# Attention and a bilinear feed-forward on one core: transposes moved from TensorE to DMA

## The chip, the cores and the metric

The kernel runs on one core of a Trainium2 chip. The metric is device time in microseconds (us), the median of several executions. The profiler takes one execution; its span is about 2 us shorter than the measured time.

## The reference

Attention with a bias from a table of relative positions, then a feed-forward layer that multiplies two projections:

```
# q, k, v: [batch 8, heads 8, seq 576, dim 64];  w_a, w_b: [512, 1536];  w_out: [1536, 512]
scores = q @ k.T / 8 + bias[head, |i - j| bucket]
x      = softmax(scores) @ v              # back to [8 * 576, 512]
out    = ((x @ w_a) * (x @ w_b)) @ w_out  # float32
```

## The kernel before

A step of the main loop handles one pair of heads: 32 pairs, four to a batch. A sequence of 576 is 512 main positions and a tail of 64. While pair `s` is computed, `quota` units of feed-forward work for an earlier batch are put between its steps. A unit is four matrix products of 512 columns (0.216 us each); 36 units make a chunk of 512 rows, one chunk to a batch and a ninth one for all tails.

Each pair needs its queries and keys with the head dimension on partitions. TensorE transposes them: four blocks and a tail block for the queries, four blocks for the keys. Five more blocks turn the output of the previous pair into the layout of the feed-forward. VectorE copies every result out of PSUM.

```python
ps_sc (2 x 2 banks: scores)   ps_av (1 bank)   ps_tr (1 bank: transposes, tail product)
ps_ff (2 banks: feed-forward)
...
def t_q(p, eng=None):
    ps = ps_tr.tile([128, 1024], BF16, tag="tr", name=f"trq{p}")
    transposes(ps, qn, p, "qr")                       # 4 blocks on TensorE
    nc.tensor.transpose(ps[:, SM:SM + 128], qkt[b % 2][:, 2 * hp:2 * hp + 2, :], ident[:, :])
    copy(eng, qT[:, 0:S], ps[:, 0:S])                 # and four small copies of tails
...
def ff_a(c, df):                                      # one unit
    pa = ps_ff.tile([128, 512], FP32, tag="ffn", name=f"pa{c}_{df}")
    ... 4 products ...
    nc.scalar.activation(out=ha[:, :], in_=pa[:, :], func=ACTF.Copy)
def ff_b(c, df):                                      # the next unit
    pb = ps_ff.tile([128, 512], FP32, tag="ffn", name=f"pb{c}_{df}")
    ... 4 products ...
    nc.vector.tensor_tensor(out=g_sb[df][:, :], in0=pb[:, :], in1=ff["ha"][:, :], op=MULT)
...
quotas = {4: 7, 5: 7, 6: 7, 7: 8, 8: 7}               # 9 from pair 9 on
# one pair (U = a unit, A = attention times values of the pair before):
[qk(s,0), ex(s,0), U, ex(s,1), A(0,1,2), U, mul(s,0), t_q(s+1), U, mul(s,1), qk(s,2), ex(s,2), U,
 ex(s,3), t_k(s+1), U, mul(s,2), A(3,4), U, mul(s,3), qk_tail(s), ex_tail(s), U, t_x(s-1), U,
 mul_tail(s), U];  v_next(s)
```

Here `qk` is scores, `ex` their exponentials (ScalarE), `mul` the multiplication by the bias factor (VectorE), `t_q`, `t_k` and `t_x` the transposes of queries, keys and outputs, and `v_next` the copy of the next values (VectorE).

The softmax here doesn't subtract the row's maximum and nothing guards it: scores larger than these inputs give would overflow.

## Time and profile before

| | before |
|---|---|
| time, median of 3 | 450.67 us (449.96 to 452.07) |
| TensorE busy | 424.7 us, 95% of the span |
| VectorE, ScalarE busy | 64%, 55% |
| period of a batch in the middle | 47.52 us |

The first fence is from the page of the kernel before: busy time by engine, then the span in 40 slices with busy shares in tenths, the granted TensorE clock, and the DMA engines.

```profile
...
PE 424.7 (95%) x3578; PEld 221.1 (49%) x3643; DVE 287.4 (64%) x838; ACT 245.8 (55%) x350; POOL 88.9 (20%) x117
...
PE   5676999999999999999999999999999999999995
...
PEclk8579999999999999999999999999999999999999
DMA  9999999420942097207912290200010002002004
...
```

TensorE is at 9 (90% or more) in nearly every slice after the first four, at full clock. The DMA engines are idle for much of the middle.

The next fence is the stretch table of the kernel before. Columns: stretch, its length, busy time (count) of TensorE, weight loads, VectorE, ScalarE, GpSimd, then clock, DMA share (packet time over the time of 16 engines; packets overlap, so it can pass 1) and GB/s.

```profile
...
0.00:20.00 20.00, 10.97 (x51) 4.12 (x52) 11.78 (x50) 9.44 (x13) 14.71 (x25) 0.70 1.07 153
20.00:40.00 20.00, 14.80 (x187) 10.48 (x188) 15.15 (x55) 14.69 (x21) 10.47 (x15) 0.78 1.37 203
40.00:75.00 35.00, 32.35 (x321) 17.58 (x326) 30.03 (x90) 22.40 (x33) 19.58 (x24) 1.00 1.68 161
...
157.00:184.00 27.00, 26.74 (x256) 14.66 (x259) 19.84 (x56) 16.01 (x22) 9.28 (x11) 1.00 0.88 75
184.00:211.00 27.00, 26.79 (x247) 14.23 (x250) 18.94 (x57) 17.14 (x24) 4.96 (x7) 1.00 0.24 40
...
```

The first 40 us are start-up, where TensorE is busy about half of the time. In the middle it is busy 26.7 of 27 us.

The timeline of TensorE in the kernel before shows what a transpose costs. Columns: start, duration, engine, line, operation, output and inputs, shapes, count.

```profile
...
189.32 0.38 PE L426 MATMUL po_3_2890<-wo,g_127 128*128 128x512 bf16 x1
189.54 0.44 PE L395 MATMUL trx_2895<-ident,XG_112 128*128 128x128 bf16 x5
189.82 0.38 PE L426 MATMUL po_3_2890<-wo,g_128 128*128 128x512 bf16 x1
...
194.86 0.39 PE L262 MATMUL trq_2986<-ident,qn_93 128*128 128x128 bf16 x4
195.08 0.22 PE L268 MATMUL trq_2986<-ident,qkt_99 128*128 128x128 bf16 x1
195.14 0.38 PE L406 MATMUL pa_1_2997<-xn_120,wa_113 128*128 128x512 bf16 x1
...
```

Read start to start, because matrix products overlap: five output transposes take TensorE from 189.54 to 189.82, 0.28 us, and four query blocks and a tail block from 194.86 to 195.14, again 0.28 us. Four key blocks take 0.22 us. There is no idle time around them. The Trainium skill's page "TensorE: Matmul & The Clock Gate" (section "Wait — 56ns, not 53.3ns?") gives 55 to 56 ns between 128-column products; this trace agrees (0.28 us for five).

### The profile page before, as it was taken

What the parts mean: (1) busy time and instruction counts of PE and PEld (TensorE: products, weight loads), DVE (VectorE), ACT (ScalarE), POOL (GpSimd) and SP (SyncE); (2) the same over time, 40 slices, a digit from 0 to 9 for tenths busy, and PEclk for the clock granted to TensorE, in tenths of its full rate; (3) what the DMA queues carried; (4) which work ended last, traced back from release to release, by engine and by line L of the source; (5) the groups of instructions that cost most, each with busy time, mean ns of one, the idle gap of its engine ahead of it and who ended that gap; (6) DMA issues with size and microseconds to landing.
All of it is one profiled execution on the core that took longest, in us unless ns stands there. A gap on an engine that the chain in (4) does not pass through costs nothing.

```text
span 449.3 us, 9012 instructions
## 1 busy us (share of the span) xinstructions
PE 424.7 (95%) x3578; PEld 221.1 (49%) x3643; DVE 287.4 (64%) x838; ACT 245.8 (55%) x350; POOL 88.9 (20%) x117
## 2 busy tenths in 40 slices
PE   5676999999999999999999999999999999999995
PEld 2264455555555555555555555555555554444442
DVE  5579789668766787577856786587658862330320
ACT  2678566556655665566556665566556652322321
POOL 9456365010801070105200350100000000000000
PEclk8579999999999999999999999999999999999999
DMA  9999999420942097207912290200010002002004
GB/s 101 219 200 203 192 148 76 82 65 1 107 72 63 15 84 72 77 25 49 104 49 54 16 137 27 76 1 1 23 71 2 1 1 94 1 0 93 1 1 94
DMA packets 87370, 30.35 MB, mean 68 GB/s; under 512 B 64760, under 2 KB 82712, under 8 KB 87328
## 3 DMA queue, kind: packets, MB, share of 16 engines
q0 software_dynamic: 80144, 18.88, 45.0%
q1 hardware_dynamic: 6992, 10.86, 7.3%
q8 instruction: 28, 0.46, 0.4%
q14 instruction: 14, 0.11, 0.1%
q10 hardware_dynamic: 192, 0.03, 0.0%
HBM read 39.18 MB, written 9.45 MB: 108 GB/s over the span
## 4 chain that ended last, share of the span: by engine, by line
PE 83%; DVE 10%; DMA 3%; issue 2%; ACT 1%; SPq 0%; DVEq 0%; ACTq 0%
DMA Wt<-bias_tab 2%; DVE XG_111 L387 1%; DVE g_125 L419 1%; DVE g_124 L419 1%; PE warm L208 1%; PE po_1_1335 L426 1%; PE po_0_1275 L426 1%; DMA bias_tab<-tab_sb 1%; PE po_1_2057 L426 1%; PE po_1_4869 L426 1%; PE po_1_3463 L426 1%; PE po_1_2760 L426 1%; PE po_1_4166 L426 1%; PE po_2_1403 L426 1%; PE po_3_6071 L426 1%
## 5 line engine op out<-in xcount | busy, mean ns | idle before, releaser
L416 PEld LDWEIGHTS <-wb_118 128*128 128x128 bf16 x144 | 12.4, 97 | 16.6 <-issue 5.6
L406 PEld LDWEIGHTS <-wa_114 128*128 128x128 bf16 x144 | 12.5, 98 | 15.3 <-issue 3.4
L416 PEld LDWEIGHTS <-wb_117 128*128 128x128 bf16 x144 | 12.4, 97 | 14.9 <-issue 4.7
L406 PEld LDWEIGHTS <-wa_113 128*128 128x128 bf16 x144 | 12.5, 98 | 14.6 <-issue 3.0
L416 PEld LDWEIGHTS <-wb_116 128*128 128x128 bf16 x144 | 12.3, 97 | 14.9 <-issue 5.1
L406 PEld LDWEIGHTS <-wa_115 128*128 128x128 bf16 x144 | 12.7, 98 | 13.4 <-issue 2.5
L123 POOL DMA_DIRECT2D qn_93<-in_q_dram x12 | 11.0, 925 | 38.6 <-PE trq_3162 L268 18.5
L123 POOL DMA_DIRECT2D qn_94<-in_q_dram x12 | 10.6, 886 | 40.2 <-PE trq_2459 L268 18.5
L146 POOL DMA_DIRECT2D vt_104<-in_v_dram x8 | 4.9, 620 | 53.7 <-PE av_3_2848 L376 17.3
L132 POOL DMA_DIRECT2D kn_95<-in_k_dram x12 | 10.6, 906 | 6.8 <-DVE qr_844 L251 6.6
L146 POOL DMA_DIRECT2D vt_103<-in_v_dram x8 | 5.0, 640 | 34.8 <-PE av_3_2145 L376 17.3
L132 POOL DMA_DIRECT2D kn_96<-in_k_dram x12 | 10.6, 912 | 0.0
L395 PEld LDWEIGHTS <-XG_112 128*128 128x128 bf16 x80 | 5.8, 98 | 5.4 <-DVE XG_112 L387 1.5
L395 PEld LDWEIGHTS <-XG_111 128*128 128x128 bf16 x80 | 5.8, 98 | 5.1 <-DVE XG_111 L387 1.8
L302 PEld LDWEIGHTS <-KT_108 64*128 64x128 bf16 x88 | 2.8, 95 | 10.7 <-issue 8.6
L419 DVE TENSOR_TENSOR g_124<-pb_0_5871,ha_0_5869 128x512 bf16<-128x512 f32 x1 | 0.7, 692 | 11.4 <-PE pb_0_5871 L416 11.4
L302 PEld LDWEIGHTS <-KT_109 64*128 64x128 bf16 x88 | 2.6, 95 | 10.4 <-issue 10.4
L426 PEld LDWEIGHTS <-g_124 128*128 128x128 bf16 x36 | 3.5, 97 | 7.0 <-issue 4.7
L302 PEld LDWEIGHTS <-KT_110 64*128 64x128 bf16 x80 | 2.4, 95 | 8.2 <-issue 8.1
L114 POOL DMA_DIRECT2D vn_98<-in_v_dram x5 | 4.2, 836 | 7.4 <-DVE vm_102 L291 6.8
L426 PEld LDWEIGHTS <-g_126 128*128 128x128 bf16 x36 | 3.5, 98 | 4.3
L426 PEld LDWEIGHTS <-g_134 128*128 128x128 bf16 x36 | 3.5, 98 | 4.3
(3194 smaller groups left out, 1643.6 us busy)
## 6 DMA issues: line engine op xcount, KB each, us to landing
qn_93<-in_q_dram POOLq DMA_DIRECT2D x16, 128.0 KB, 4.2
kn_95<-in_k_dram POOLq DMA_DIRECT2D x16, 128.0 KB, 5.1
qn_94<-in_q_dram POOLq DMA_DIRECT2D x16, 128.0 KB, 5.4
kn_96<-in_k_dram POOLq DMA_DIRECT2D x16, 128.0 KB, 4.9
wo<-in_moe_w_out_dram POOLq DMA_DIRECT2D x1, 1536.0 KB, 16.4
vn_97<-in_v_dram POOLq DMA_DIRECT2D x3, 512.0 KB, 7.1
vn_98<-in_v_dram POOLq DMA_DIRECT2D x3, 512.0 KB, 5.8
vn_97<-in_v_dram POOLq DMA_DIRECT2D x2, 256.0 KB, 10.7
```

Source lines behind the costliest of these rows:

```text
L114: nc.gpsimd.dma_start(out=dst[:, 256 * h0:256 * h1].rearrange("p (h x) -> p h x", x=256), in_=src[b, h0:h1, 0:SM, :].rearrange("h (p t) d ...
L123: nc.gpsimd.dma_start(out=qn[b % 2][:, :].rearrange("p (t h d) -> p t h d", h=H, t=NM)[:, t, h0:h1, :], in_=q[b, h0:h1, 128 * t:128 * t + ...
L132: nc.gpsimd.dma_start(out=kn[b % 2][:, :].rearrange("p (t h d) -> p t h d", h=H, t=NM)[:, t, h0:h1, :], in_=k[b, h0:h1, t:SM:NM, :].transp ...
L146: nc.gpsimd.dma_start(out=vt[b % 2][64 * hh:64 * hh + 64, :, hh, 0:Dh], in_=v[b, hh:H:2, SM:S, :].transpose([1, 0, 2]))
L208: nc.tensor.matmul(out=warm[:, :], lhsT=zero_sb[:, 0:128], rhs=zero_sb[:, :], start=True, stop=True)
L302: nc.tensor.matmul(out=ps[:, hh, :], lhsT=kT[r, 128 * t:128 * t + 128], rhs=qT[r, 0:SM], start=True, stop=True)
L387: nc.vector.tensor_tensor(out=xg[0:np_, j0:j0 + n, :, :], in0=pav[0:np_, s0:s0 + n, :, 0:Dh], in1=rc.unsqueeze(3).to_broadcast([np_, n, 2, ...
L395: nc.tensor.transpose(ps[:, 128 * jq:128 * jq + 128], XG[p % 2][:, jq, :, :], ident[:, :])
L406: nc.tensor.matmul(out=pa[:, :], lhsT=wa_sb[df // 4][:, mc, 128 * (df % 4):128 * (df % 4) + 128], rhs=xn_sb[mc][:, 512 * c:512 * c + 512], ...
L416: nc.tensor.matmul(out=pb[:, :], lhsT=wb_sb[df // 4][:, mc, 128 * (df % 4):128 * (df % 4) + 128], rhs=xn_sb[mc][:, 512 * c:512 * c + 512], ...
L419: nc.vector.tensor_tensor(out=g_sb[df][:, :], in0=pb[:, :], in1=ff["ha"][:, :], op=MULT)
L426: nc.tensor.matmul(out=po[:, :], lhsT=g_sb[df][:, 128 * tt:128 * tt + 128], rhs=wo_sb[:, df, :], start=(df == 0), stop=(df == NDF - 1))
```

## The change

The intent is to take nine transposes a pair (from batch 2 on) and five output transposes (pairs 4 to 30) off TensorE, and their copies off VectorE. The DMA's transposes do them from SBUF to SBUF. Queries and keys go in units of four heads; outputs go pair by pair. The output stores move from SyncE's queue to ScalarE's, so that SyncE's queue only has transposes. The first two batches stay on TensorE.

```diff
+    def t_half(b, g):
+        for dst, src in ((KB, kn), (QB, qn)):
+            nc.sync.dma_start_transpose(out=dst[i][:, g, ...], in_=src[i][:, 1024 * g:1024 * g + 1024])
+        if g == 0:
+            nc.sync.dma_start_transpose(out=ZB[i]..., in_=tl[i]...)      # tails of the whole batch
 ...
     def t_x(p, eng=None):
+        if 4 <= p < NP - 1:
+            nc.sync.dma_start_transpose(out=xn_sb[hp][:, SM * b:SM * b + SM]..., in_=XG[p % 2][:, 0:4, ...])
+            nc.sync.dma_start_transpose(out=xn_sb[hp][:, c0:c0 + ST], in_=XG[p % 2][0:ST, 4, ...])
+            return
 ...                                   # qk_tail: the 64 x 64 tail product becomes two products
-    nc.sync.dma_start(out=out[r0:r0 + 128, :], in_=ob[:, :])
+    nc.scalar.dma_start(out=out[r0:r0 + 128, :], in_=ob[:, :])
 ...                                   # early pairs: tails transposed in the keys' bank; tail loads 2 -> 4
-    quotas = {4: 7, 5: 7, 6: 7, 7: 8, 8: 7}
+    quotas = {4: 7, 5: 7, 6: 7, 7: 7, 8: 6}
 ...                                   # new order of a pair's steps:
+    [qk(s,0), ex(s,0), U, ex(s,1), A(0,1,2), U, mul(s,0), t_q(s+1), U, mul(s,1), A(3,4), qk(s,2), ex(s,2), U,
+     ex(s,3), t_k(s+1), U, t_x(s-1), mul(s,2), U, mul(s,3), U, qk_tail(s), ex_tail(s), U, U, mul_tail(s)]; v_next(s)
 ...
+        if s % 4 == 2 and b < B: t_half(b, 0)                 # two pairs before use
+        if s % 4 == 0 and 2 <= b - 1 < B: t_half(b - 1, 1)
```

More of the change, by code (lines that the diff above doesn't have):

```diff
@@ L91 @@
     vn = [wpool.tile([128, H * NM * Dh], BF16, name=f"vn{i}") for i in range(2)]
-    qkt = [wpool.tile([128, H, Dh], BF16, name=f"qkt{i}") for i in range(2)]
+    tl = [wpool.tile([128, H // 2, 2, 128], BF16, name=f"tl{i}") for i in range(2)]
     vm = [wpool.tile([128, H, NM, Dh + 1], BF16, name=f"vm{i}") for i in range(2)]
     vt = [wpool.tile([128, H // 2, 2, Dh + 1], BF16, name=f"vt{i}") for i in range(2)]
-    QT = [wpool.tile([128, S + 2 * ST], BF16, name=f"QT{i}") for i in range(3)]
-    KT = [wpool.tile([128, SM + 2 * ST], BF16, name=f"KT{i}") for i in range(3)]
+    QT = [wpool.tile([128, NM, 128], BF16, name=f"QT{i}") for i in range(2)]
+    KT = [wpool.tile([128, NM, 128], BF16, name=f"KT{i}") for i in range(2)]
+    ZT = [wpool.tile([128, 2, 128], BF16, name=f"ZT{i}") for i in range(2)]
+    QB = [wpool.tile([128, 2, NM, 2, 128], BF16, name=f"QB{i}") for i in range(2)]
+    KB = [wpool.tile([128, 2, NM, 2, 128], BF16, name=f"KB{i}") for i in range(2)]
+    ZB = [wpool.tile([128, H // 2, 2, 128], BF16, name=f"ZB{i}") for i in range(2)]
     XG = [wpool.tile([128, 5, 2, Dh], BF16, name=f"XG{i}") for i in range(2)]
@@ L123, in load_q @@
             nc.gpsimd.dma_start(
-                out=qn[b % 2][:, :].rearrange("p (t h d) -> p t h d", h=H, t=NM)[:, t, h0:h1, :],
+                out=by_tile(qn[b % 2])[:, h0 // 4, t, :, :],
                 in_=q[b, h0:h1, 128 * t:128 * t + 128, :].transpose([1, 0, 2]))
@@ L132, in load_k, with by_tile @@
             nc.gpsimd.dma_start(
-                out=kn[b % 2][:, :].rearrange("p (t h d) -> p t h d", h=H, t=NM)[:, t, h0:h1, :],
+                out=by_tile(kn[b % 2])[:, h0 // 4, t, :, :],
                 in_=k[b, h0:h1, t:SM:NM, :].transpose([1, 0, 2]))
+    def by_tile(x):
+        return x[:, :].rearrange("p (g t h d) -> p g t h d", g=2, h=H // 2, t=NM)
     def load_v(b, h0, h1):
@@ L139, in load_tails @@
     def load_tails(b):
-        for src, o in ((q, 0), (k, 64)):
-            nc.gpsimd.dma_start(out=qkt[b % 2][o:o + 64, :, :],
-                                in_=src[b, :, SM:S, :].transpose([1, 0, 2]))
+        for i, src in enumerate((q, k)):
+            for hh in range(2):
+                nc.gpsimd.dma_start(
+                    out=tl[b % 2][64 * hh:64 * hh + 64, :, i, Dh * hh:Dh * hh + Dh],
+                    in_=src[b, hh:H:2, SM:S, :].transpose([1, 0, 2]))
     def load_vt(b):
@@ L148, in load_vt, with load_half @@
                 in_=v[b, hh:H:2, SM:S, :].transpose([1, 0, 2]))
+    def load_half(b, g):
+        if b >= B:
+            return
+        load_k(b, 4 * g, 4 * g + 4)
+        load_q(b, 4 * g, 4 * g + 4)
+        if g == 0:
+            load_tails(b)
+        load_v(b, 4 * g, 4 * g + 4)
     def load_w_in(part):
@@ L166 @@
     nc.vector.memset(zero_sb[:, :], 0.0)
+    for i in range(2):
+        nc.vector.memset(tl[i][0:64, :, :, Dh:], 0.0)
+        nc.vector.memset(tl[i][64:128, :, :, 0:Dh], 0.0)
     for i in range(2):
@@ L228 @@
                                               ap=[[1, 64], [2 * TB, H // 2], [1, 192]]))
-    for i in range(3):
-        nc.vector.memset(QT[i][0:64, S + ST:], 0.0)
-        nc.vector.memset(QT[i][64:128, S:S + ST], 0.0)
-        nc.vector.memset(KT[i][0:64, SM + ST:], 0.0)
-        nc.vector.memset(KT[i][64:128, SM:SM + ST], 0.0)
     st = [dict() for _ in range(NP)]
@@ L255, in reorder, with transposes @@
             st[p][tag] = r
-    def transposes(ps, src, p, tag):
-        b, hp = divmod(p, 4)
+    def transposes(ps, p, tag):
         for t in range(NM):
-            x = (st[p][tag][:, t, :, :] if early(b) else
-                 src[b % 2][:, 512 * t + 128 * hp:512 * t + 128 * hp + 128])
-            nc.tensor.transpose(ps[:, 128 * t:128 * t + 128], x, ident[:, :])
+            nc.tensor.transpose(ps[:, 128 * t:128 * t + 128], st[p][tag][:, t, :, :], ident[:, :])
     def t_q(p, eng=None):
@@ L265, in t_q @@
         b, hp = divmod(p, 4)
+        if p >= NP or not early(b):
+            return
         ps = ps_tr.tile([128, 1024], BF16, tag="tr", name=f"trq{p}")
-        transposes(ps, qn, p, "qr")
-        nc.tensor.transpose(ps[:, SM:SM + 128], qkt[b % 2][:, 2 * hp:2 * hp + 2, :], ident[:, :])
-        qT, kT = QT[p % 3], KT[p % 3]
-        if early(b):
-            copy(eng, qT[:, 0:SM].rearrange("d (p t) -> d p t", t=NM),
-                 ps[:, 0:SM].rearrange("d (t p) -> d p t", t=NM))
-            copy(eng, qT[:, SM:S], ps[:, SM:S])
-        else:
-            copy(eng, qT[:, 0:S], ps[:, 0:S])
@@ L276, in t_q @@
-        for hh in range(2):
-            r = slice(64 * hh, 64 * hh + 64)
-            nc.vector.tensor_copy(out=kT[r, SM + ST * hh:SM + ST * hh + ST], in_=ps[r, S:S + ST])
-            nc.vector.tensor_copy(out=qT[r, S + ST * hh:S + ST * hh + ST], in_=ps[r, SM:S])
+        transposes(ps, p, "qr")
+        copy(eng, QT[p % 2][:, :, :].rearrange("d a c -> d (a c)").rearrange("d (p t) -> d p t", t=NM),
+             ps[:, 0:SM].rearrange("d (t p) -> d p t", t=NM))
     def t_k(p, eng=None, pool=None, tag="tr"):
@@ L282, in t_k @@
         b, hp = divmod(p, 4)
+        if p >= NP or not early(b):
+            return
         ps = (pool or ps_tr).tile([128, 1024], BF16, tag=tag, name=f"trk{p}")
-        transposes(ps, kn, p, "kr")
-        copy(eng, KT[p % 3][:, 0:SM], ps[:, 0:SM])
-        st[p]["at"] = [None] * NM
+        transposes(ps, p, "kr")
+        for i in range(2):
+            nc.tensor.transpose(ps[:, SM + 128 * i:SM + 128 * i + 128], tl[b % 2][:, hp, i, :],
+                                ident[:, :])
+        copy(eng, KT[p % 2][:, :, :], ps[:, 0:SM].rearrange("d (t c) -> d t c", t=NM))
@@ new lines, in t_k @@
+        copy(eng, ZT[p % 2][:, :, :], ps[:, SM:SM + 256].rearrange("d (i c) -> d i c", i=2))
+    def t_half(b, g):
+        i = b % 2
+        for dst, src in ((KB, kn), (QB, qn)):
+            nc.sync.dma_start_transpose(
+                out=dst[i][:, g, :, :, :].rearrange("d t h c -> d (t h) c"),
+                in_=src[i][:, 1024 * g:1024 * g + 1024])
+        if g == 0:
+            nc.sync.dma_start_transpose(
+                out=ZB[i][:, :, :, :].rearrange("d h i c -> d (h i) c"),
+                in_=tl[i][:, :, :, :].rearrange("p h i x -> p (h i x)"))
@@ L288, in v_in, with operands @@
+    def operands(p):
+        b, hp = divmod(p, 4)
+        if early(b):
+            return QT[p % 2][:, :, :], KT[p % 2][:, :, :], ZT[p % 2][:, :, :]
+        g, e = divmod(hp, 2)
+        return QB[b % 2][:, g, :, e, :], KB[b % 2][:, g, :, e, :], ZB[b % 2][:, hp, :, :]
     def v_in(b, h0, h1):
@@ L296, in qk @@
     def qk(p, t0):
-        qT, kT = QT[p % 3], KT[p % 3]
+        qT, kT, _ = operands(p)
+        st[p].setdefault("at", [None] * NM)
         for t in (t0, t0 + 1):
@@ L301, in qk @@
                 r = slice(64 * hh, 64 * hh + 64)
-                nc.tensor.matmul(out=ps[:, hh, :], lhsT=kT[r, 128 * t:128 * t + 128],
-                                 rhs=qT[r, 0:SM], start=True, stop=True)
+                nc.tensor.matmul(out=ps[:, hh, :], lhsT=kT[r, t, :], rhs=qT[r, :, :],
+                                 start=True, stop=True)
             st[p]["ps", t] = ps
@@ L318, in qk_tail @@
     def qk_tail(p):
-        hp = p % 4
-        qT, kT = QT[p % 3], KT[p % 3]
+        qT, kT, z = operands(p)
         ps = ps_sc.tile([128, 2, 512], FP32, tag="sc", name=f"qkt{p}")
@@ L324, in qk_tail @@
                 out=ps[:, 0, :].rearrange("p (h t c) -> p h t c", h=2, t=NM)[:, :, t, :],
-                lhsT=kT[:, 128 * t:128 * t + 128], rhs=qT[:, S:S + 2 * ST],
-                start=True, stop=True)
-        nc.tensor.matmul(out=ps[:, 1, :], lhsT=kT[:, SM:SM + 2 * ST], rhs=qT[:, 0:SM],
-                         start=True, stop=True)
+                lhsT=kT[:, t, :], rhs=z[:, 0, :], start=True, stop=True)
+        nc.tensor.matmul(out=ps[:, 1, :], lhsT=z[:, 1, :], rhs=qT, start=True, stop=True)
         pt = ps_tr.tile([128, 512], FP32, tag="tr", name=f"qktt{p}")
-        nc.tensor.matmul(out=pt[:, 0:ST], lhsT=kT[:, SM:SM + 2 * ST], rhs=qT[:, SM:S],
-                         start=True, stop=True)
+        for hh in range(2):
+            nc.tensor.matmul(out=pt[:, 0:ST], lhsT=z[:, 1, :], rhs=z[:, 0, ST * hh:ST * hh + ST],
+                             start=(hh == 0), stop=(hh == 1))
         st[p]["ps"] = (ps, pt)
@@ L392, in t_x @@
         b, hp = divmod(p, 4)
+        if 4 <= p < NP - 1:
+            nc.sync.dma_start_transpose(
+                out=xn_sb[hp][:, SM * b:SM * b + SM].rearrange("d (j c) -> d j c", j=4),
+                in_=XG[p % 2][:, 0:4, :, :].rearrange("p j h d -> p (j h d)"))
+            c0 = SM * B + ST * b
+            nc.sync.dma_start_transpose(
+                out=xn_sb[hp][:, c0:c0 + ST],
+                in_=XG[p % 2][0:ST, 4, :, :].rearrange("p h d -> p (h d)"))
+            st[p].clear()
+            return
         ps = ps_tr.tile([128, 1024], BF16, tag="tr", name=f"trx{p}")
@@ L436, in ff_o @@
                     r0 = S * (2 * tt + hh) + SM
-                    nc.sync.dma_start(out=out[r0:r0 + ST, :], in_=ob[64 * hh:64 * hh + 64, :])
+                    nc.scalar.dma_start(out=out[r0:r0 + ST, :], in_=ob[64 * hh:64 * hh + 64, :])
     units = []
@@ L493 @@
         v_next(s)
-    quotas = {4: 7, 5: 7, 6: 7, 7: 8, 8: 7}
+    load_half(2, 0)
+    load_half(2, 1)
+    quotas = {4: 7, 5: 7, 6: 7, 7: 7, 8: 6}
     for s in range(4, NP + 1):
@@ L509 @@
         elif new:
-            steps += [U, lambda: ex(s, 1), A(0, 1, 2), U, lambda: mul(s, 0)]
-            if s + 1 < NP:
-                steps += [lambda: t_q(s + 1)]
-            steps += [U, lambda: mul(s, 1), lambda: (qk(s, 2), ex(s, 2)), U, lambda: ex(s, 3)]
-            if s + 1 < NP:
-                steps += [lambda: t_k(s + 1)]
-            steps += [U, lambda: mul(s, 2), A(3, 4), U, lambda: mul(s, 3),
-                      lambda: (qk_tail(s), ex_tail(s)), U, lambda: t_x(s - 1), U,
-                      lambda: mul_tail(s), U]
+            steps += [U, lambda: ex(s, 1), A(0, 1, 2), U, lambda: mul(s, 0), lambda: t_q(s + 1), U,
+                      lambda: mul(s, 1), A(3, 4), lambda: (qk(s, 2), ex(s, 2)), U,
+                      lambda: ex(s, 3), lambda: t_k(s + 1), U, lambda: t_x(s - 1),
+                      lambda: mul(s, 2), U, lambda: mul(s, 3), U,
+                      lambda: (qk_tail(s), ex_tail(s)), U, U, lambda: mul_tail(s)]
         else:
@@ L522 @@
         b = s // 4 + 1
-        if s > 4 and s % 4 == 1 and b < B:
-            load_q(b, 0, 8)
-            load_k(b, 0, 8)
-            load_tails(b)
-            load_v(b, 0, 8)
+        if s % 4 == 2 and b < B:
+            t_half(b, 0)
+        if s % 4 == 0 and 2 <= b - 1 < B:
+            t_half(b - 1, 1)
+        if s % 4 == 1 and 2 <= b < B:
             load_vt(b)
+        if s % 4 == 3:
+            load_half(b + 1, 0)
+        if s % 4 == 1 and b > 2:
+            load_half(b, 1)
         quota = quotas.get(s, 9)
```

## The prediction

> **What bounds the kernel now.** The first 75 us are start-up: the stretch table gives TensorE 11.0 of 20, 14.8 of 20 and 32.4 of 35 us busy, and the chain of waits there goes through the bias table's transfers and TensorE's waits for reordered queries. From 75 to 425 us TensorE is busy 99% at full clock, and the waits of TensorE show almost nothing. VectorE is busy 64% and ScalarE 55% of the span. So the middle is bound by TensorE's issue. One batch takes 47.5 us (first output product of successive chunks at 130.6, 178.1, 225.6 us), 11.9 us a pair of heads. The timeline gives one pair's issue time: 9 feed-forward units of four 512-column products at 0.216 us, 7.8; scores 0.9; tails 0.5; attention times values 5 x 0.32 = 1.6; transposes 0.28 (queries and tail) + 0.22 (keys) + 0.28 (output) = 0.78; about 0.4 of small gaps.
>
> **What goes.** In pairs 8 to 31, nine transposes each: 24 x 0.50 = 12.0 us of TensorE. In pairs 4 to 30, five output transposes: 27 x 0.28 = 7.6 us. All of it lies in the TensorE-bound stretch. VectorE also loses some 2.1 us of PSUM copies a pair (0.45, 0.42, 0.52 and four of about 0.18), which is off the path.
>
> **What comes.** One more 64-column tail product per pair, 32 x 0.03 = 1.0 us; one more transpose in the eight early pairs, 0.4 us. ScalarE gets 40-odd store issues; with over 40% idle it can take them. Per batch SyncE issues five 128x1024 transposes and four pairs of 128x512 and 64x128: 58 blocks of 128x128, 1.9 MB. The trace before has no DMA transpose. The Trainium skill's page "DMA: Bandwidth & Descriptors" (section Latency and other measured facts) gives 261 GB/s for one kernel's transposes, from which I estimate 7 us a batch; its page "VectorE: DVE Perf Modes" (section The three transpose paths) gives 1309 ns for one block, which one after the other would be 76 us a batch, too slow for a 44 us batch. I believe blocks of one DMA overlap. The stretch table has the DMA engines busy some 7 us in 48, so there is room. Distance: the input transposes are issued about two pairs (22 us) ahead of use. The last output transpose of a batch has an estimated 7 us before its chunk starts; if it lands later, TensorE stalls once a batch, up to some microseconds.
>
> **Sum.** 450.7 - 19.6 + 1.4 = 432.5. I add 1.5 us for short waits on the output transposes and dearer tail loads at the start: **434 us**, 8 in 10 between 428 and 452. Faster by over 2%: 0.72; within 2%: 0.15; slower: 0.13.
>
> **What would show it.** TensorE's instructions fall by about 320 and its busy time by 17 to 19 us; it stays above 97% busy from 75 to 425 us; the period of a batch falls from 47.5 to 44.5 us; VectorE's busy time falls by some 55 us; start-up up to 75 us and the last 75 us of pure feed-forward stay within 1 to 2 us. Transposes should land in under 7 us and the waits of TensorE should name no transposed tile (query, key or xn tiles).
>
> **What would make it wrong.** Transposes that take 10 us or more each, or occupy SyncE's queue one after the other: then TensorE waits at each chunk start for xn, or at the first pair of a unit for its queries and keys, and the gain is eaten or reversed. Transposes colliding with the bursts of 128-byte input packets. Stores on ScalarE holding back the exponentials or the evictions between feed-forward units, so that TensorE waits for PSUM. Slower start-up from the tails' four DMAs and extra memsets.

## The result

| | before | after |
|---|---|---|
| time, median of 4 | 450.31 us (449.13 to 452.07) | 439.56 us (438.61 to 440.27) |
| span of the profiled run | 449.3 us | 438.3 us |
| TensorE busy, records | 424.7 us, 3578 | 409.7 us, 3279 |
| VectorE busy | 287.4 us | 242.9 us |
| period of a batch in the middle | 47.52 us | 45.33 us |

The ratio is 0.9757 (95% interval 0.9717 to 0.9797). A ratio here is the mean time of one kernel's runs over that of the other's of the same rounds, so it is not quite the ratio of the medians quoted.

The page of the changed kernel, the same rows:

```profile
...
PE 409.7 (93%) x3279; PEld 207.1 (47%) x3332; DVE 242.9 (55%) x597; ACT 249.7 (57%) x353; POOL 130.0 (30%) x187
...
PE   6475899999999999999999999999999999999995
...
PEclk9769999999999999999999999999999999999999
DMA  8999999999639982899079905960320012002004
...
```

The stretch table of the changed kernel:

```profile
...
0.00:20.00 20.00, 10.26 (x54) 4.20 (x54) 10.36 (x34) 9.60 (x13) 14.62 (x25) 0.89 0.98 145
20.00:40.00 20.00, 14.74 (x186) 10.45 (x187) 12.56 (x37) 14.22 (x22) 12.02 (x17) 0.77 1.33 187
40.00:75.00 35.00, 31.67 (x323) 17.74 (x327) 28.77 (x77) 22.78 (x33) 22.76 (x32) 1.00 1.60 163
...
157.00:184.00 27.00, 26.48 (x224) 13.31 (x225) 17.57 (x42) 17.13 (x23) 3.45 (x6) 1.00 0.44 63
184.00:211.00 27.00, 26.79 (x216) 13.20 (x218) 15.86 (x39) 17.82 (x26) 13.59 (x20) 1.00 1.30 132
...
```

TensorE is still busy 26.5 to 26.8 of 27 us in the middle. The busy share thus hides what was lost. A product of 0.38 us starts every 0.216 us, so a gap of 0.15 us between two issues makes no hole in the busy time.

The next table splits the span at the start of chosen pairs' first exponential on ScalarE, read from the traces. The expected column uses the prediction's own terms: -0.28 us for an output, -0.50 for queries and keys, +0.03 for a tail product, +0.05 for an early pair's added transpose, and 0.86 for each of the two feed-forward units that the quotas move to the end.

| from pair to pair | before | after | change | expected |
|---|---|---|---|---|
| start to 4 | 42.88 | 44.21 | +1.33 | +0.4 |
| 4 to 8 | 43.98 | 42.42 | -1.56 | -1.9 |
| 8 to 9 | 10.38 | 9.52 | -0.86 | -1.6 |
| 9 to 12 | 35.59 | 34.58 | -1.01 | -2.25 |
| 12 to 28, four batches | 190.09 | 181.29 | -8.80 | -12.0 |
| 28 to 31 | 35.48 | 33.69 | -1.79 | -2.25 |
| 31 to the end | 90.90 | 92.59 | +1.69 | +1.5 |

Some 7 us of the expected gain are missing. The largest part is in the middle, 0.8 us a batch; most of the rest is in the start (0.9 us) and in pairs 8 to 12 (2.0 us). The missing part of the middle can be seen in the timeline of TensorE in the changed kernel:

```profile
...
193.41 0.38 PE L446 MATMUL pa_1_2832<-xn_128,wa_119 128*128 128x512 bf16 x1
193.62 0.38 PE L446 MATMUL pa_1_2832<-xn_129,wa_119 128*128 128x512 bf16 x1
193.99 0.38 PE L456 MATMUL pb_1_2842<-xn_126,wb_122 128*128 128x512 bf16 x1
194.20 0.38 PE L456 MATMUL pb_1_2842<-xn_127,wb_122 128*128 128x512 bf16 x1
...
```

The products start every 0.216 us, but from 193.62 to 193.99 there are 0.37 us. `pb_1` needs the PSUM bank of `pb_0`, and VectorE frees it, as its timeline shows:

```profile
...
193.25 0.69 DVE L459 TENSOR_TENSOR g_130<-pb_0_2824,ha_0_2790 128x512 bf16<-128x512 f32 x1 [0.70 <-PE pb_0_2824 L456]
...
```

This multiplication ends at 193.94, and `pb_1` starts at 193.99. Three such gaps of 0.15 us come in a batch. In the kernel before, transposes or score products stood between such units and covered that wait. A second kind of gap comes once a batch, from 210.72 to 211.15:

```profile
...
210.72 0.22 PE L397 MATMUL av_0_3072<-vt_103,att_3021 128*128 128x130 bf16 x1
211.15 0.19 PE L406 MATMUL av_0_3072<-vm_101,at_0_2893 128*128 128x65 bf16 x1 [0.20 <-DVE vm_101 L322]
211.18 0.20 PE L406 MATMUL av_0_3072<-vm_101,at_1_2901 128*128 128x65 bf16 x1
...
```

Here TensorE waits for the copy of the values (`vm`), which the new order leaves behind the tail's multiplication at the end of the pair.

I summed the distance from each product's start to the next, less its nominal issue time, over pairs 12 to 28. Holes of exactly one missing record were left out. Of all kinds of gap, two grew: first to second projection (`pa` to `pb`) from 0.00 to 0.45 us a batch, and inside attention times values from 0.35 to 0.71. Together that is 0.81 us, the amount missing: 3.0 - 0.8 = 2.2 = 47.52 - 45.33.

### The profile page after: what moved, and what is told of

It is laid out like the page before. It is cut to its first block, busy times and chain, and to the rows that moved or that the text cites. A ratio compares the mean times of both kernels' runs of the same rounds, so it can differ in the third digit from the quotient of the medians.

```text
span 438.3 us, 8493 instructions
## 1 busy us (share of the span) xinstructions
PE 409.7 (93%) x3279; PEld 207.1 (47%) x3332; DVE 242.9 (55%) x597; ACT 249.7 (57%) x353; POOL 130.0 (30%) x187
## 2 busy tenths in 40 slices
DMA packets 137449, 42.18 MB, mean 96 GB/s; under 512 B 114840, under 2 KB 132792, under 8 KB 137408
## 4 chain that ended last, share of the span: by engine, by line
PE 84%; DVE 3%; issue 1%; ACT 1%; ACTq 0%; DVEq 0%
DVE g_137 L459 1%; PE po_2_5590 L466 1%; PE po_0_1287 L466 1%; PE po_0_4447 L466 1%; PE po_0_3198 L466 1%; PE po_0_2567 L466 1%; PE po_0_1936 L466 1%; PE po_0_3829 L466 1%; PE po_3_3974 L466 1%; PE po_3_2712 L466 1%; PE po_3_3343 L466 1%; PE po_3_4592 L466 1%; PE po_3_2081 L466 1%; PE po_3_5607 L466 1%; PE po_0_5556 L466 1%
## 5 line engine op out<-in xcount | busy, mean ns | idle before, releaser
L157 POOL DMA_DIRECT2D vt_104<-in_v_dram x8 | 4.9, 623 | 64.3 <-PE av_3_2636 L406 27.7
L456 PEld LDWEIGHTS <-wb_123 128*128 128x128 bf16 x144 | 13.8, 97 | 18.2 <-issue 3.8
L446 PEld LDWEIGHTS <-wa_119 128*128 128x128 bf16 x144 | 14.0, 98 | 17.3 <-issue 1.0
L456 PEld LDWEIGHTS <-wb_122 128*128 128x128 bf16 x144 | 12.4, 97 | 19.3 <-issue 8.5
L446 PEld LDWEIGHTS <-wa_121 128*128 128x128 bf16 x144 | 13.4, 98 | 17.2 <-issue 2.5
L157 POOL DMA_DIRECT2D vt_103<-in_v_dram x8 | 5.1, 648 | 55.0 <-PE av_3_3267 L406 27.3
L456 PEld LDWEIGHTS <-wb_124 128*128 128x128 bf16 x144 | 12.5, 97 | 17.6 <-issue 6.5
L128 POOL DMA_DIRECT2D qn_93<-in_q_dram x24 | 18.2, 820 | 7.3 <-DMA wo<-in_moe_w_out_dram 6.4
L446 PEld LDWEIGHTS <-wa_120 128*128 128x128 bf16 x144 | 12.5, 98 | 15.2 <-issue 3.2
L137 POOL DMA_DIRECT2D kn_95<-in_k_dram x24 | 18.2, 803 | 4.2 <-issue 2.5
L128 POOL DMA_DIRECT2D qn_94<-in_q_dram x24 | 18.2, 811 | 1.4 <-DMA vn_97<-in_v_dram 0.8
L137 POOL DMA_DIRECT2D kn_96<-in_k_dram x24 | 18.1, 796 | 0.3 <-issue 0.3
L466 PEld LDWEIGHTS <-g_134 128*128 128x128 bf16 x36 | 3.5, 97 | 8.7 <-issue 6.8
L119 POOL DMA_DIRECT2D vn_97<-in_v_dram x8 | 6.5, 810 | 0.7 <-DVE g_132 L459 0.7
L119 POOL DMA_DIRECT2D vn_98<-in_v_dram x8 | 6.3, 783 | 0.9 <-DMA qn_94<-in_q_dram 0.6
L334 PEld LDWEIGHTS <-KB_113 64*128 64x128 bf16 x96 | 2.9, 94 | 7.5 <-issue 6.4
L151 POOL DMA_DIRECT2D tl_100<-in_q_dram x8 | 5.0, 632 | 4.0 <-DMA vn_97<-in_v_dram 3.3
L231 PE MATMUL warm<-zero_sb 128*128 128x512 bf16 x10 | 4.6, 629 | 1.2 <-DVE zero_sb L186 1.2
L466 PEld LDWEIGHTS <-g_130 128*128 128x128 bf16 x36 | 3.5, 98 | 4.6 <-DMA qn_94<-in_q_dram 0.4
L466 PEld LDWEIGHTS <-g_137 128*128 128x128 bf16 x36 | 3.5, 98 | 4.3
L466 PEld LDWEIGHTS <-g_136 128*128 128x128 bf16 x36 | 3.5, 98 | 4.3
```

Of the source, the lines that this page charges most:

```text
L119: nc.gpsimd.dma_start(out=dst[:, 256 * h0:256 * h1].rearrange("p (h x) -> p h x", x=256), in_=src[b, h0:h1, 0:SM, :].rearrange("h (p t) d ...
L128: nc.gpsimd.dma_start(out=by_tile(qn[b % 2])[:, h0 // 4, t, :, :], in_=q[b, h0:h1, 128 * t:128 * t + 128, :].transpose([1, 0, 2]))
L137: nc.gpsimd.dma_start(out=by_tile(kn[b % 2])[:, h0 // 4, t, :, :], in_=k[b, h0:h1, t:SM:NM, :].transpose([1, 0, 2]))
L151: nc.gpsimd.dma_start(out=tl[b % 2][64 * hh:64 * hh + 64, :, i, Dh * hh:Dh * hh + Dh], in_=src[b, hh:H:2, SM:S, :].transpose([1, 0, 2]))
L157: nc.gpsimd.dma_start(out=vt[b % 2][64 * hh:64 * hh + 64, :, hh, 0:Dh], in_=v[b, hh:H:2, SM:S, :].transpose([1, 0, 2]))
L231: nc.tensor.matmul(out=warm[:, :], lhsT=zero_sb[:, 0:128], rhs=zero_sb[:, :], start=True, stop=True)
```

## The experiments

The theory before the experiments: the removed transposes had partly stood in time in which TensorE would have waited anyway, mainly for the two feed-forward banks, and partly for exponentials and copies; start-up was lost to ScalarE's extra copies. Rivals: the stores hold back ScalarE; the DMA transposes load SyncE's queue or the DMA engines to their limit; the new order of steps costs time by itself.

Periods and stretches below are from the same stretch points as in the table above. Times are medians; ratios are against the kernel before in the same rounds.

| run | time, us | ratio | start to 4 | 8 to 12 | batch period | 31 to end |
|---|---|---|---|---|---|---|
| before | 450.31 | 1 | 42.88 | 45.97 | 47.52 | 90.90 |
| after | 439.56 | 0.9757 | 44.21 | 44.10 | 45.33 | 92.59 |
| dummy_pe | 459.06 | 1.0194 | 45.07 | 46.59 | 48.01 | 92.79 |
| ring3 | 432.49 | 0.9605 | 41.82 | 43.65 | 44.88 | 89.20 |
| stores_sync | 438.72 | 0.9744 | 44.07 | 43.41 | 45.33 | 92.66 |
| zt_vector | 439.96 | 0.9768 | 44.71 | 44.10 | 45.33 | 92.58 |
| before_ring3 | 445.97 | 0.9910 | 41.47 | 45.97 | 47.52 | 87.56 |
| order_only | 463.73 | 1.0295 | 41.02 | 48.80 | 49.25 | 91.30 |
| inputs_only | 447.62 | 0.9937 | 43.51 | 44.77 | 46.00 | 93.18 |
| twice_dma | 440.30 | 0.9783 | 43.59 | 44.10 | 45.33 | 92.58 |
| best1 | 430.62 | 0.9554 | 43.35 | 43.29 | 44.52 | 88.78 |
| best1q | 428.41 | 0.9516 | 41.45 | 43.90 | 44.52 | 87.05 |
| best1s | 429.89 | 0.9537 | 42.83 | 42.60 | 44.52 | 88.86 |
| best1qs | 431.86 | 0.9602 | 42.18 | 45.37 | 44.52 | 87.14 |

The start scatters by up to 1.9 us between runs of equal code: order_only has the start of the kernel before and took 41.02 against 42.88 us. The period of a batch repeats to 0.01 us, so it is the better witness.

### dummy_pe: the transposes put back as idle work

```diff
+    def dummy(name, n):
+        ps = ps_tr.tile([128, 1024], BF16, tag="tr", name=name)
+        for i in range(n):
+            nc.tensor.transpose(ps[:, 128 * i:128 * i + 128], ident[:, :], ident[:, :])
     # t_q and t_k of pairs from 8 on: dummy 5 and 4; t_x of pairs 4 to 30: dummy 5, and the DMA transposes as well
```

> The changed kernel with the removed TensorE transposes put back as work without purpose (same counts at the same places, result never copied), the DMA transposes kept. Theory (the removed transposes partly stood in time in which TensorE waits anyway for a feed-forward PSUM bank or a tail's exponential): the batch period rises from 45.3 by only some 2.2 us to 47.5, total about 452 less the start, 450 to 453. Rival (transposes cost their full issue time of 3.0 us a batch, and something new, DMA or ScalarE's stores, slows the changed kernel): the period rises by 3.0 to 48.3 us and the total to 457 to 459.

The period rose by 2.68 us, to 48.01, and the total to 459.06 us. The transposes' issue time is 3.12 us a batch (4 x 0.78), so 0.44 us of them is hidden. That lies between the theory's 2.2 and the rival's 3.0 and settles less than hoped. It says that about half of the missing 0.8 us is hidden time, and the other half something else that is new. In this run's trace the gap between the first and the second projection is 0.00 again, and the wait for the copied values is still there.

### ring3 and before_ring3: a third bank for the feed-forward

```diff
-    ps_tr = ... tile_pool(name="ps_tr", bufs=1, space=PSUM)
-    ps_ff = ... tile_pool(name="ps_ff", bufs=2, space=PSUM)
+    ps_ff = ... tile_pool(name="ps_ff", bufs=3, space=PSUM)      # all users of ps_tr take a turn in this ring
```

> The changed kernel with the one PSUM bank of the transposes joined to the two feed-forward banks in one ring of three. Theory (waits for an eviction before the next feed-forward product): the gaps of about 0.15 us between a product of the first weight and the next of the second vanish, the period of a batch falls from 45.3 to 44.6 to 44.9 us, and the last 75 us of pure feed-forward fall by about 3 us (24 gaps of 0.14); start-up also a little better because the tail product no longer waits for the key's copy in the same bank; total 431 to 435. Rival (DMA or stores hold TensorE): period stays 45.3 and total at 436 to 440.

> The kernel before with its transposes' PSUM bank joined to the two feed-forward banks in one ring of three. Theory (in the kernel before, transposes between the feed-forward units cover the waits for a feed-forward bank, so a third bank has little to give there; only the pure feed-forward end gains): batch period 47.2 to 47.6 us against 47.5, the end from pair 31 about 3.3 us shorter, total 444.5 to 447.5. Rival (the third bank is worth the same 0.45 us a batch with or without transposes, which then hid nothing): period 47.0 to 47.1 us.

In the changed kernel the ring took 0.45 us off each batch, 3.4 us off the end and 2.4 us off the start, some of which may be scatter: 432.49 us. In the kernel before it took 3.3 us off the end and nothing off the period, 47.52 in both. So the same third bank is worth 0.45 us a batch only once the transposes have gone. The timeline of TensorE in ring3 shows products of both projections without a gap (names carry no numbers in the traces of the experiments):

```profile
...
189.69 1.03 PE L445 MATMUL pa<-xn,wa 128*128 128x512 bf16 x4
190.55 1.03 PE L455 MATMUL pb<-xn,wb 128*128 128x512 bf16 x4
191.41 1.03 PE L445 MATMUL pa<-xn,wa 128*128 128x512 bf16 x4
192.28 0.39 PE L353 MATMUL qkt<-ZB,KB 128*128 128x128 bf16 x4
...
```

Groups of four start every 0.86 us, four times 0.216. The Trainium skill's page "Perfetto Trace Analysis" (section Matmuls) says that independent groups of products should rotate through different PSUM banks so that the eviction of one overlaps the next. Two banks were enough where 0.28 us of other TensorE work stood among three units in a row.

### inputs_only: output transposes back on TensorE

```diff
-        if 4 <= p < NP - 1:
+        if False:
```

> The changed kernel with output transposes back on TensorE and VectorE, input transposes by DMA kept. Full issue time: period 45.3 + 4 x 0.28 = 46.4 us. Theory (a part of it falls into waits that are there anyway): 46.1 to 46.4 us, total 444 to 446.5.

The period is 46.00, just under the expected range. Four output transposes of 0.28 us issue for 1.12 us, and cost 0.67. The difference of 0.45 us is the gap between the projections, which is 0.00 in this trace. In the new order `t_x` stands right between two units. The total, 447.62 us, lies above its range: in pairs 5 and 6, where the keys are still transposed by TensorE, output transposes wait 0.9 and 1.2 us for the bank that they share with the keys.

### stores_sync: stores back on SyncE's queue

```diff
-                nc.scalar.dma_start(out=out[r0:r0 + 128, :], in_=ob[:, :])      # and the tails' stores
+                nc.sync.dma_start(out=out[r0:r0 + 128, :], in_=ob[:, :])
```

> The changed kernel with stores back on SyncE's queue. Rival (the 0.34 us of each store issue on ScalarE hold back exponentials): pairs that store get shorter, total 437 or less. Theory (stores on ScalarE cost next to nothing): no gain from it; since a store waits for ScalarE in SyncE's queue ahead of transposes, equal or slower, 439 to 443.

The period is the same, so stores on ScalarE are no part of the 0.8 us. The run was still 0.84 us faster by the medians. Its trace has 0.69 us less between pairs 8 and 12, and 0.36 less between 4 and 8. There the changed kernel's waits of TensorE (engine, line and what waited, the releaser, then total, times, longest) show tail exponentials that come late:

```profile
...
PE qk_1_1473 L334 <- ACT att_1447 L369: 0.6, 1, 0.6
...
PE qk_1_1334 L334 <- ACT att_1318 L369: 0.6, 1, 0.6
...
PE av_0_1810 L406 <- DVE vm_101 L322: 0.2, 1, 0.2
...
```

`att` is the tail's exponential of the pair before. ScalarE's timelines show why it is late, first in the changed kernel, then in stores_sync:

```profile
...
84.57 0.60 ACT L470 ACTIVATE ob_0_1306<-po_0_1287 128x512 f32<-128x512 f32 x1 [0.97 <-PE po_0_1287 L466]
85.20 0.36 ACTq L473 DMA_DIRECT2D out_dram<-ob_0_1306  x1
85.61 0.22 ACT L368 ACTIVATE att_1318<-qktt_1315 128x64 bf16<-128x64 f32 x1 [0.43 <-ACT ob_0_1306 L470]
...
```

```profile
...
84.44 0.60 ACT L470 ACTIVATE ob<-po 128x512 f32<-128x512 f32 x1 [0.97 <-PE po L466]
84.94 0.22 ACT L368 ACTIVATE att<-qktt 128x64 bf16<-128x64 f32 x1
...
```

The store waits for the copy of `ob` and is issued before the exponential, which starts 1.04 us after the copy's start, against 0.50 without the store. From start to start TensorE loses 0.75 us at pair 8 and 0.78 at pair 9 in the changed kernel, and nothing and 0.25 in stores_sync. So stores on ScalarE do hold back an exponential where the two meet. My statement that moving stores back gains nothing missed this part. The intervals of the two ratios overlap, so the total alone would not show it.

### zt_vector: the start

```diff
-        copy(eng, ZT[p % 2][:, :, :], ps[:, SM:SM + 256]...)     # eng is ScalarE for pairs 1 to 4
+        copy(None, ZT[p % 2][:, :, :], ps[:, SM:SM + 256]...)    # VectorE
```

> The changed kernel with the copy of the early pairs' transposed tails on VectorE instead of ScalarE. Theory (the start-up loss of 1.3 us by pair 4 comes from this copy queued on ScalarE before the tail product): the first score product of pair 4 starts at 42.3 to 42.8 us instead of 43.5, waits of the tail product for ScalarE's copy fall from 3.4 us to under 1.5, total 438.3 to 439. Rival (dearer loads of tails, or the second tail transpose): pair 4 stays at 43.3 to 43.6 us.

Pair 4 starts at 44.71 against 44.21 us by its first exponential (44.01 against 43.51 by its first score product, outside both ranges), and the waits of the tail product stay (2.7 us, now for VectorE). My explanation by ScalarE's queue falls. In ring3 the tail product has another bank than the keys and does not wait. The five runs of changed kernels with the ring reached pair 4 at 41.5 to 43.4 us, the six without it at 43.5 to 45.1, so part of the loss goes with the shared bank. Also, the first load of values is issued by GpSimd at 8.20 us instead of 6.93, behind four tail loads instead of two. No run takes that away alone, so the split of the start's loss stays open.

### order_only: the new order without the new transposes

```diff
 # before.py with the step list of after.py, transposes on TensorE, quotas unchanged
```

> The kernel before with only the new order of steps inside a pair (last attention tiles before the second half of the scores, the output transposes earlier, the tail's multiplication last), transposes still on TensorE, quotas as before. The run with transposes put back as idle work had a period of 48.0 us against 47.5 before, of which 0.12 is the added tail product. If the new order is what costs the rest, the period is 47.8 to 47.9 us and the total 452 to 454; if stores on ScalarE or the DMA transposes cost it, the period stays 47.4 to 47.6.

I expected 47.8 to 47.9, and it was 49.25 us. The waits of this run's TensorE (names merged, so more than one tile to a row):

```profile
...
PE trx L399 <- DVE KT L242: 8.7, 14, 1.7
...
PE av L380 <- DVE vm L295: 1.2, 6, 0.2
...
```

The new order puts the output transposes right behind those of the keys. With both on TensorE they share one bank, and the outputs wait for the keys' copy, 8.7 us in all. This wait makes 1.37 of the 1.73 us by which the period grew between pairs 12 and 28, so the run does not test the order of steps alone. Such a wait can't happen in the changed kernel from batch 2 on. What it does share with the changed kernel is the wait for the copied values, 1.2 us in all, 0.2 us by this view six times (the full gap is 0.36 us). The kernel before has none. So that wait comes from the order of steps, not from the DMA.

### twice_dma: the input transposes issued twice

```diff
-        for dst, src in ((KB, kn), (QB, qn)):
+        for dst, src in ((KB, kn), (QB, qn)) * 2:
```

> The changed kernel with every 128x1024 query and key transpose issued twice into the same place (16 of the batch's blocks of 128x128 become 48 in all, the second waits for the first). Theory (DMA transposes are off the critical path, with slack): period 45.3 to 45.5 us, total 438 to 440.5, no wait of TensorE on a transposed tile. Rival (SyncE's queue or the DMA engines are close to their limit): TensorE waits for xn or key tiles, period over 46 us.

The period did not move by 0.01 us. The DMA queues of the changed kernel and of this run (queue, kind, packets, MB, share of 16 engines' span) show that the work was really done:

```profile
...
q1 hardware_dynamic: 50704, 13.28, 19.9%
...
```

```profile
...
q1 hardware_dynamic: 76048, 19.57, 27.9%
...
KB<-kn SPq DMA_TRANSPOSE x24, 3.6
QB<-qn SPq DMA_TRANSPOSE x24, 3.3
...
```

No product of TensorE waits on a transposed tile in either. This rules out the DMA engines and SyncE's queue as a limit of the changed kernel's middle. (The block counts in the expectation are a slip: a batch has 32 blocks of queries and keys, which became 64.)

### best1, best1q, best1s, best1qs: the remedies together

```diff
 # best1: ring3, and in the list of steps
-                      lambda: (qk_tail(s), ex_tail(s)), U, U, lambda: mul_tail(s)]
+                      lambda: (qk_tail(s), ex_tail(s)), U, lambda: mul_tail(s), lambda: v_next(s), U]
 # best1q: and
-    quotas = {4: 7, 5: 7, 6: 7, 7: 7, 8: 6}
+    quotas = {4: 7, 5: 7, 6: 7, 7: 8, 8: 7}
 # best1s: best1 and the stores on SyncE;  best1qs: all of it
```

> The changed kernel with both found remedies: one ring of three PSUM banks, and the tail's multiplication and the copy of the next values issued one feed-forward unit earlier in each pair. Theory: the remaining wait of 0.36 us a batch for the copied values goes, period 44.88 to 44.5 us, total 429.5 to 431.5. If that wait is not from the order of steps, the period stays 44.9 and the total 432 to 433.

> The same with the feed-forward quotas of the kernel before in pairs 7 and 8, so that each chunk starts two units (1.7 us) earlier after its last output transpose. Theory (the last transpose of a batch lands well before use): no wait for xn, the two waits for a tail's exponential at pairs 8 and 9 shrink, 0 to 1 us faster than without. Rival (the smaller quotas were needed for the transpose to land): each batch gets a wait for xn of 0.5 us or more, period over 45 us, total 433 or more.

> The first of these three with stores on SyncE's queue. The earlier run with stores moved back won 0.9 us in pairs 4 to 9 and nothing later; theory: the same here, 0.5 to 1 us faster than with ScalarE's stores, period of a batch the same. If it depended on the two-bank waits, no difference or slower.

> All four edits together: the ring of three banks, the earlier multiplication and copy, the old quotas, and stores on SyncE's queue. If the gain of the stores' move at pairs 4 to 9 came from ScalarE being late with a tail's exponential there, the old quotas have already removed the two waits and the move adds under 0.5 us: 427.5 to 429. If the two gains are separate they add: 427 to 428. Period of a batch 44.5 us either way.

best1 has a period of 44.52 us, 3.0 us under the kernel before, which is the whole of the predicted gain; the gap inside attention times values is 0.35 us again, as before. best1q has the lowest median: 428.41 us (427.91 to 431.21), a ratio of 0.9516 to the kernel before. That is 2.2 us under best1, more than expected, but not clear of it: the 95% intervals of the ratios overlap (0.9474 to 0.9558 and 0.9526 to 0.9583), and 1.9 of the 3.2 us between the two traces lie before pair 4, where the code is the same. Its quotas let each chunk start two units earlier, and there is no wait for `xn`, so the smaller quotas of the change were not needed there; the two waits for a tail's exponential are gone.

best1s is 0.73 us under best1 by the medians, as expected, with overlapping intervals. Its trace has the same period and, as in stores_sync, 0.37 us less between pairs 4 and 8 and 0.69 less between 8 and 12.

best1qs missed its range. Adding SyncE's stores to the old quotas made it slower, 431.86 us (ratio 0.9571 to 0.9633, clear of best1q), with this wait of TensorE:

```profile
...
PE pa L445 <- DMA xn<-XG: 1.8, 1, 1.8
...
```

SyncE's timeline in best1qs shows why:

```profile
...
87.12 5.19 SPq L472 DMA_DIRECT2D out_dram<-ob  x2
92.40 1.22 SPq L423 DMA_TRANSPOSE xn<-XG  x1
93.71 1.18 SPq L427 DMA_TRANSPOSE xn<-XG  x1
...
```

The first row stands for two stores. The second waits in the queue for ScalarE's copy of its tile, which ends at 91.95, and only then can the output transpose behind it issue, at 92.40, although VectorE has finished the four blocks that it reads at 90.29. In best1q the same transpose is issued at 89.60, as soon as those blocks are done, and lands in time. Either the small quotas or ScalarE's stores give that transpose room; one of them is enough, and without both the first DMA-fed chunk starts 1.8 us late. This happened once, at pair 9, and not in later batches. It explains some 1.5 of the 2.8 us between the traces of best1q and best1qs; 0.7 are in the start, and 0.5 between pairs 28 and 31 stay open.

## Why the prediction was right or wrong

The prediction was faster, 434 us, between 428 and 452. Measured were 439.56 us. The direction and the mechanism held; the size was off: a gain of 10.8 us instead of 16.7.

- **What bounds the kernel: right.** Between pairs 12 and 28, TensorE's issue and the two gaps explain the change of the period to a few hundredths of a microsecond.
- **What goes, 19.6 us at full issue time: mis-sized.** This term, "All of it lies in the TensorE-bound stretch", is the step that failed. Transposes by their start-to-start time are 3.12 us a batch; taking out the four output transposes gave 0.67 instead of 1.12 us (inputs_only against after), and all of them together 2.68 instead of 3.12 (dummy_pe), because units that then adjoin wait for a bank. The third bank shows it: 0.45 us a batch without the transposes, 0.00 with them.
- **The reordering was not costed.** The prediction said nothing of the new order of steps. It adds a gap of 0.36 us a batch (order_only has the wait too, best1 removes it), and at pairs 8 and 9 TensorE waits about 0.6 us each for a tail's exponential that stands behind a store on ScalarE; the old quotas (best1q) or stores on SyncE (stores_sync, best1s) undo most of that.
- **Start-up: 1.5 us added for it and for waits on outputs.** The start lost 1.33 us in this pair of traces, with a scatter of up to 1.9 us. There were no waits on outputs, so that 1.5 us fits the start is luck.
- **DMA: right in what matters for the time, wrong in two figures.** Median landings of 128x1024 query and key transposes are 3.3 to 5.8 us, of the outputs 2.4 to 5.9 us. No product of TensorE waits on a transposed tile, nor when the input transposes are doubled. But 7 of 73 recorded landings took over 7 us, the longest 9.1. And "busy some 7 us in 48" is not what the stretch table gives: the DMA share from 130.6 to 178.1 us is 0.57, which is 27 us of packet time for each engine.
- **Stores on ScalarE: right for the middle**, where moving them back changes nothing, and wrong by some 0.7 us for pairs 8 to 12, where store issues hold back two exponentials, as the prediction's last paragraph feared.
- **Signs named.** Period 45.33 instead of 44.5; TensorE's busy time fell 15.0 instead of 17 to 19 us and VectorE's 44.5 instead of 55; the busy share stayed high, and so told little.

With the two remedies in the middle the period is 44.52, so nothing else is missing there.

## What to carry to other kernels

Work on the bounding engine is worth its issue time only if its neighbours do not then wait for the same buffer: before removing filler, compute how long the buffer behind it takes to come free, and add a buffer with the change. Read start-to-start distances and a period that repeats, not busy shares, and try the added buffer on the old kernel too: no gain there and a gain here shows that the filler hid a wait. When several orderings are changed along with the main idea, cost them as well, and test them one at a time, since two that are each harmless can cost time together.

## What the Trainium skill lacked or had wrong

- "VectorE: DVE Perf Modes" (section The three transpose paths) gives 1309 ns for one 128x128 DMA transpose and does not say how several blocks add up. Here eight blocks in one DMA landed after 3.3 to 6.5 us (medians by tile), latency included, 0.4 to 0.8 us a block.
- "DMA: Bandwidth & Descriptors" (section Latency and other measured facts) gives 261 GB/s. From that I estimated 7 us a batch. From 174 to 177 us of the changed kernel, when a key and a query transpose move and little else, the stretch table shows 175 GB/s; at that rate a batch's 1.9 MB would take 10.9 us (an estimate). Whether the issue of the transposes or the DMA engines set that rate is not shown.
- "Advanced Engine Details and Errata" (section X-Bar Transpose (TRN2)) says that transposes are as fast as regular DMAs; no run here compares the two on the same bytes.
- No page that I found states for trn2 how long the issue of a DMA transpose holds its queue: in the changed kernel a transpose holds SyncE's for 1.1 us or more (median 1.2), and a store holds ScalarE's for 0.34 us or more.
